# Moving a gather, a transposition, a few sums and one buffer across the seam between attention and a mixture of experts

## The chip, the cores and the metric

The kernel runs on one core of one Trainium2 chip. The metric is the device time of one execution in microseconds (us), the median of several runs. Times inside the execution come from one profiled run and count from its first instruction. The engines are called PE (TensorE; PEld is its weight load), DVE (VectorE), ACT (ScalarE), POOL (GpSimd) and SP (SyncE, which here only issues transfers).

## The reference

Attention without a softmax, then an RMS norm, then a mixture of experts in which each token goes to one of eight experts or is passed through unchanged.

```python
batch, n_heads, seq, head_dim = (8, 8, 576, 64)
kv = np.einsum('bhsd,bhse->bhde', k, v)
out = np.einsum('bhsd,bhde->bhse', q, kv)
rms = np.sqrt(np.mean(out * out, axis=-1, keepdims=True) + 1e-06)
attn = (out / rms * g_norm).astype(np.float32)
...
x = np.ascontiguousarray(attn.transpose(0, 2, 1, 3)).reshape(B * S, H * D)   # 4608 x 512
skip_score = x @ w_skip
do_compute = skip_score > 0
logits = xc @ w_gate
e_idx = np.argmax(logits, axis=1)
...
h = np.maximum(xc[mask] @ w1[e], 0.0)          # w1[e]: 512 x 1024, e of 8
y[mask] = gate_w[mask, None] * (h @ w2[e])     # w2[e]: 1024 x 512
out[do_compute] = xc + y
```

## The kernel before

**Attention.** The queries are worked through in 36 units. A unit is a batch b, a group i of four of the nine row columns of that batch, and a half u of the eight heads; the ninth columns of four batches together make two further units (i is `None`; these are units 16, 17 and, at the very end, 34, 35). The loop `for n in range(NU + 2)` is software-pipelined and written out by hand under a manual schedule, so each engine gets its instructions in the order of the code. In step n it turns the queries of unit n + 1 (`turn`, L432, bank `q_ps`), takes the root for unit n - 1 (`root`, L497, on ACT), multiplies unit n (`values`, L468 or L476, into a bank pair `o_ps`, or `sum_ps` for units 28, 31 and 34) and squares it (L482, ACT), sums the squares (`squares`, L490, DVE), and normalises unit n - 1 (`norm`: reciprocal L504, product `xl` L508, both DVE). Then `finish` gives POOL the small gate sums `lp` and `lg` (L525, L529, L533: skip score and eight logits of each token, carried through as nine extra columns) and puts the large product with g, `xb` (L538), into a list `late`. `scale` empties that list one step later, so in POOL's order xb(n) stands just before lp(n + 1); each xb waits for the reciprocal of the unit after it. `store_x` sends a finished xb to the output in HBM, half by POOL (L560, L566) and half by SP (L561, L570) for some groups, all by SP for the others. Jobs can be hung on a step with `at(step, part, job)`; the parts are "early", "pe", "dve" and "end".

**Ranking.** The tokens are ranked in three groups of tiles that end at 12, 22 and 36. For each group `choose` (DVE, L582 to L602) finds the expert of each token as a one-hot `ohb`, `rank` (PE, L612 to L618) counts, and `number` (DVE, L629 to L644) makes slot numbers: the high part `hi_k` and a one-hot of the low part, `oha_k`. After the second group the experts are ordered by how many tokens they have, and the weights of the first one are loaded (SP, L309 and L314). `columns` (DVE: `ohc` L659, `bv` L663) makes from `hi_k` the columns that `place` (PE, L672) multiplies with `oha_k`, so that each slot gets its token's row number in `srow`.

**The first slots.** The tokens of groups one and two come from batches 0 to 4, so the first 128 slots of the first expert are known before attention ends. `early` computes them: L757, L761 on DVE, 22 products on PE (L767, the job `put`), three small DVE operations (L771 to L776), and a gather of 128 rows from the output by POOL (L778) into `xg0`. It is a generator driven by the loop: `put` runs in the "pe" part of step 30, and the rest is issued in the "dve" part of that step.

**After attention** the pools of the attention are closed and the experts' pools opened on the same memory; a tile there waits for what used its room before. `bank` hands out seven PSUM banks in turn. The code at the seam is this:

```python
        expert_in(xg0, xt0, first)
        layer_1(0, xt0, ht0, slice(0, P), range(0, 5))
        rank(LAST)
        drain(number(LAST))
        layer_1(0, xt0, ht0, slice(0, P), range(5, FC))
        last_bv = columns(NE, NT - NE, colid_i, row_k, 2, slot_pool, NT // 2)
        settle(0, NE, first_bv)
        yps0 = layer_2(0, ht0, first, None, range(0, 3))
        settle(NE, NT, last_bv)
        layer_2(0, ht0, first, yps0, range(3, 5))
```

`expert_in` turns the 128 rows (L971 on PE, L974 on ACT), `layer_1` and `layer_2` are the expert's two products (L995, L1006; eight blocks each), and `settle` is `place` and two DVE additions (L735). With `srow` complete, POOL gathers the other rows of the first two experts (L961), PE repeats some slots (L914) and turns the rows, and the experts run one after another to the end: the first with plain products, the other seven with a seven-product scheme (L1074). SP loads the next expert's weights as rooms come free, POOL scatters the results (L1216).

## Time and profile before

| | us |
|---|---|
| runs | 400.13, 400.14, 398.63; median 400.13 |
| profiled execution, its own time | 399.31 |
| its span, first to last instruction | 397.4 |
| PE busy | 365.8 (92% of the span) |
| PEld, DVE, ACT, POOL busy | 317.8, 240.7, 144.0, 124.9 |
| mean granted PE clock | 0.973 |
| last attention product ends (L476) | 118.25 |
| first expert product begins (L995) | 122.56 |
| last slot products begin (L672, 14 of them) | 137.40 |
| first late gather begins (L961) | 139.04 |
| rest of layer one of the first expert begins | 145.94 |

A profile line in order of time has the start, the busy time, the engine, the line and operation, what is written from what, and in brackets how long the engine had been idle and what ended that ("<-"). If an instruction waits for several things, the profile names the one that came last by its records. The granted clock is the share of full speed at which PE was let run. The time of the execution exceeds the span by 1.9 us.

### The profile page before, as it was taken

To read this page: it belongs to the slowest core of one execution; us is meant where nothing else is said; L and a number is where in the kernel's file an instruction comes from. 1 tells how busy PE (TensorE), PEld (TensorE's weight loads), DVE (VectorE), ACT (ScalarE), POOL (GpSimd) and SP (SyncE) were. 2 spreads that over 40 slices of the span, in tenths; PEclk is the share of its full clock that TensorE was granted. 3 is DMA by queue.
4 is the path that set the end of the run, shared out by engine and by line. 5 is a ranking of instruction groups with operands and counts; after the bars stand their busy time and mean duration, and the time that the engine had idled before them with its cause. 6 is when DMAs were issued, how large, how long until landed. Compare 5 with 4: busy or idle time off the path is not lost.

```text
span 397.4 us, 9594 instructions
## 1 busy us (share of the span) xinstructions
PE 365.8 (92%) x3822; PEld 317.8 (80%) x3822; DVE 240.7 (61%) x615; ACT 144.0 (36%) x384; POOL 124.9 (31%) x197
## 2 busy tenths in 40 slices
PE   8789999899967889999999999999999989989991
PEld 4577988799857659579879978978988978979980
DVE  2333567577884651656756657857767756868711
ACT  2265786576862212113402421421431430421410
POOL 7023677565776270133012303203303203102001
PEclk9699999999996989999999999999999999999997
DMA  8999999985795249726516354663663572611001
GB/s 296 395 391 389 343 408 403 405 262 178 239 389 142 54 136 383 262 65 228 183 73 225 105 211 116 210 225 105 206 228 104 185 246 67 210 47 55 2 2 50
DMA packets 31544, 81.70 MB, mean 206 GB/s; under 512 B 2106, under 2 KB 2114, under 8 KB 31492
## 3 DMA queue, kind: packets, MB, share of 16 engines
q1 hardware_dynamic: 27456, 68.69, 49.6%
q0 software_dynamic: 4016, 12.31, 9.1%
q8 instruction: 32, 0.52, 0.6%
q14 instruction: 20, 0.16, 0.1%
q10 hardware_dynamic: 20, 0.02, 0.0%
HBM read 66.80 MB, written 14.48 MB: 205 GB/s over the span
## 4 chain that ended last, share of the span: by engine, by line
PE 56%; issue 17%; DMA 12%; POOL 5%; DVE 5%; ACT 2%; POOLq 0%; DVEq 0%; ACTq 0%
PE bank L1074 23%; DMA out_dram<-xg,rows 8%; PE bank L1006 6%; PE o_ps L468 6%; PE sum_ps L352 4%; PE q_ps L432 4%; PE bank L995 3%; DMA xg<-out_dram,asrc 2%; POOL xb L538 2%; PE g_ps L366 2%; DMA xg<-out_dram,src 2%; POOL out_dram L1216 1%; DVE xl L508 1%; PE bank L971 1%; POOL xg L961 1%
## 5 line engine op out<-in xcount | busy, mean ns | idle before, releaser
L1084 ACT COPY p<-bank 128x128 f32<-128x128 f32 (+6 forms) x70 | 20.8, 297 | 105.4 <-PE bank L1074 103.8
L1074 PE MATMUL bank<-xt,w 128*128 128x128 f32 (+5 forms) x336 | 55.5, 288 | 0.0
L538 POOL TENSOR_TENSOR xb<-xl,g_b 128x512 f32<-128x512 f32 x36 | 42.9, 1191 | 31.8 <-DVE rs L504 27.9
L1074 PEld LDWEIGHTS bank<-xt,w 128*128 128x128 f32 x336 | 47.0, 190 | 1.9 <-DVE bank L1078 1.2
L1078 DVE TENSOR_TENSOR bank<-bank,p 128x128 f32<-128x128 f32 (+6 forms) x70 | 23.6, 337 | 39.8 <-PE bank L1074 38.1
L1216 POOL DMA_INDIRECT out_dram<-xg,rows x16 | 16.2, 1013 | 76.9 <-DVE xg L1213 75.4
L468 PE MATMUL o_ps<-kvd,qT 128*128 128x146 f32 x240 | 36.2, 291 | 2.5 <-DVE xl L508 2.2
L1074 PE MATMUL bank<-xs,s 128*128 128x128 f32 (+5 forms) x224 | 36.7, 288 | 0.0
L1006 PE MATMUL bank<-w,ht 128*32 128x128 f32 (+2 forms) x448 | 36.6, 322 | 0.0
L468 PEld LDWEIGHTS o_ps<-kvd,qT 128*128 128x128 f32 x240 | 31.8, 190 | 4.1 <-ACT sq L482 1.6
L961 POOL DMA_INDIRECT xg<-out_dram,src x15 | 16.8, 1122 | 51.7 <-DMA out_dram<-xg,rows 29.0
L1216 POOL DMA_INDIRECT out_dram<-xg,arows x8 | 9.0, 1128 | 76.4 <-DVE xg L1213 76.1
L1074 PEld LDWEIGHTS bank<-xs,s 128*128 128x128 f32 x224 | 31.1, 190 | 1.0 <-ACT p L1084 0.8
L490 DVE TENSOR_REDUCE rs<-sq 128x8 f32<-128x512 f32 x36 | 24.5, 679 | 11.6 <-ACT sq L482 11.5
L1006 PEld LDWEIGHTS bank<-w,ht 128*32 128x32 f32 (+2 forms) x448 | 20.4, 121 | 13.6 <-issue 10.9
L508 DVE TENSOR_TENSOR xl<-o_ps,rs 128x584 f32<-128x584 f32 x33 | 25.3, 767 | 4.3 <-PE o_ps L468 0.5
L1074 PE MATMUL bank<-w,ht 128*128 128x256 f32 x112 | 27.2, 386 | 0.0
L1074 PE MATMUL bank<-t,ht 128*128 128x256 f32 x112 | 27.1, 385 | 0.0
L352 PE MATMUL sum_ps<-v,k 64*64 64x64 f32 x1152 | 25.3, 230 | 1.6 <-issue 1.5
L352 PEld LDWEIGHTS sum_ps<-v,k 64*64 64x64 f32 x1152 | 21.8, 141 | 4.7 <-issue 2.9
L1074 PE MATMUL bank<-t,hs 128*128 128x256 f32 x112 | 25.3, 379 | 0.0
L995 PE MATMUL bank<-xt,w 128*128 128x128 f32 (+1 forms) x128 | 23.2, 349 | 1.0 <-ACT xt L974 0.7
(199 smaller groups left out, 673.6 us busy)
## 6 DMA issues: line engine op xcount, KB each, us to landing
w<-in_moe_w_dram SPq DMA_DIRECT2D x16, 2048.0 KB, 10.5
q<-in_q_dram SPq DMA_DIRECT2D x8, 1152.0 KB, 9.2
k<-in_k_dram SPq DMA_DIRECT2D x7, 1152.0 KB, 12.7
v<-in_v_dram SPq DMA_DIRECT2D x7, 1152.0 KB, 13.4
out_dram<-xb SPq DMA_DIRECT2D x26, 256.0 KB, 8.7
out_dram<-xb POOLq DMA_DIRECT2D x10, 256.0 KB, 6.7
k<-in_k_dram SPq DMA_DIRECT2D x2, 576.0 KB, 5.2
v<-in_v_dram SPq DMA_DIRECT2D x2, 576.0 KB, 6.2
```

Of the source, the lines that this page charges most:

```text
L352: nc.tensor.matmul(out=sum_ps[w * 64:(w + 1) * 64, a, u, :], lhsT=kt[r, 2 * u + w, c, :], rhs=vt[r, 2 * u + w, c, :], start=(c == 0), stop ...
L468: nc.tensor.matmul(out=ps[:, w, 0:2 * PK].rearrange("p (r k) -> p r k", r=2)[:, :, cols], lhsT=qT[:, w, a, :], rhs=kvds[b % KVD][:, u, w, ...
L490: nc.vector.tensor_reduce(out=rs[:, :, :], in_=sq[:, :, :, :].rearrange("p x y (a d) -> p x (y a) d", a=2), axis=AX.X, op=ALU.add)
L508: nc.vector.tensor_tensor(out=xl[:, :, :, :].rearrange("p x y (a k) -> p x (y a) k", a=2), in0=ps[:, :, 0:2 * PK].rearrange("p x (h k) -> ...
L538: late.append((lambda: nc.gpsimd.tensor_tensor(out=xb[:, :, 4 * u * D:(4 * u + 4) * D].rearrange("p r (w x) -> p r w x", w=2), in0=xl[:, : ...
L961: nc.gpsimd.indirect_dma_start(out=x_of(xg, off, m), out_offset=None, in_=cut_rows(m)[:, :], in_offset=bass.IndirectOffsetOnAxis(ap=idx[:, ...
L995: nc.tensor.matmul(out=hps[:, cols], lhsT=w_sb[r][0][:, dc, f * P:(f + 1) * P], rhs=xt[:, dc, cols], start=(dc == 0), stop=(dc == DC - 1))
L1006: nc.tensor.matmul(out=yps[q * m:(q + 1) * m, 0:n], lhsT=ht[:, f, off:off + m], rhs=w_sb[r][1][:, f, q * n:(q + 1) * n], start=(f == 0), s ...
L1074: nc.tensor.matmul(out=out, lhsT=lhsT(i), rhs=rhs(i), start=start and i == 0, stop=i == k - 1, skip_group_check=True)
L1078: nc.vector.tensor_tensor(out=to, in0=x, in1=y, op=ALU.add)
L1084: nc.scalar.copy(out=t, in_=x)
L1216: ins = nc.gpsimd.indirect_dma_start(out=cut_rows(m)[:, :], out_offset=bass.IndirectOffsetOnAxis(ap=rows[:, col:col + 1], axis=0), in_=x, ...
```

## The change

Six things are edited.

1. The DVE operations and the POOL gather of `early` go into the job `put`, and `put` runs in a new part "mid" of step 30: right after `values`, ahead of `squares` and `norm`.
2. `expert_in` for the first slots goes. A job `first_in` at the end of step 35 turns the 128 rows into the bank `q_ps` and copies them to a tile of their own, `xt_first`, which layer one reads. Three banks are drawn and left unused before layer one. A block of zeros moves from its own tile into the first weights' room.
3. `norm` of the last unit no longer calls `scale`, so xb(34) comes after the gate sums of unit 35 on POOL. The last two xb now wait for the end of `choose` (`ohb`) instead of the reciprocal and `bv`.
4. `columns` is split into `hits` and `weighed`; for the first 22 tiles `hits` runs before `choose`, `weighed` after it.
5. Three stores move from POOL to SP: those of units 16 and 17, of the last batch's second group (32, 33), and of units 34 and 35.
6. The last columns (`last_bv`) are written into the pool `gat_pool`, in the tiles of the first columns, after `settle` of the first 22 tiles, instead of into `slot_pool` before it.

```diff
@@ -502,7 +502,8 @@
         nq, b, i, u = units[n]
         (ps, _), rs = ops.pop(n), rss.pop(n)
         inverse = nc.vector.reciprocal(out=rs[:, :, :], in_=rs[:, :, :])
-        scale(n, inverse)
+        if n < NU - 1:
+            scale(n, inverse)
         r4 = rs[:, :, :].unsqueeze(3)
         xl = att_pool.tile([P, 2, 2, PK], FP32, tag="xl", name="xl", bufs=4)
         nc.vector.tensor_tensor(
@@ -557,21 +558,24 @@
         xb = xbs.pop(nq)
         if i is None:
             rows = out.rearrange("(f hf r p c) d -> f hf p r c d", f=NF, hf=2, r=2, c=C)[b]
-            nc.gpsimd.dma_start(out=rows[0, :, :, C - 1, :], in_=xb[0:64, :, :])
-            return lambda: nc.sync.dma_start(out=rows[1, :, :, C - 1, :], in_=xb[64:128, :, :])
+            def store():
+                for hf in range(2):
+                    nc.sync.dma_start(out=rows[hf, :, :, C - 1, :], in_=xb[hf * 64:(hf + 1) * 64, :, :])
+            return store
         rows = out[b * S:(b + 1) * S, :].rearrange("(p c) d -> p c d", c=C)[:, 4 * i:4 * i + 4, :]
         rows = rows.rearrange("p (hf r) d -> hf p (r d)", hf=2)
         x = xb[:, :, :].rearrange("p r d -> p (r d)")
-        if i == 1:
+        first = int(i == 1 and b < B - 1)
+        if first:
             nc.gpsimd.dma_start(out=rows[0], in_=x[0:64, :])
 
         def store():
-            for hf in range(i, 2):
+            for hf in range(first, 2):
                 nc.sync.dma_start(out=rows[hf], in_=x[hf * 64:(hf + 1) * 64, :])
         return store
 
 
-    ohbs, rks = {}, {}
+    ohbs, rks, chosen = {}, {}, []
 
     def choose(g):
 
@@ -599,8 +603,9 @@
                                        op0=ALU.is_gt, op1=ALU.mult)
         yield
         ohb = gat_pool.tile([P, TG, E], BF16, tag="ohb", name="ohb")[:, 0:nt, :]
-        nc.vector.tensor_tensor(out=ohb, in0=eorder[:, :].unsqueeze(1).to_broadcast([P, nt, E]),
-                                in1=fi.unsqueeze(2).to_broadcast([P, nt, E]), op=ALU.is_equal)
+        chosen.append(nc.vector.tensor_tensor(
+            out=ohb, in0=eorder[:, :].unsqueeze(1).to_broadcast([P, nt, E]),
+            in1=fi.unsqueeze(2).to_broadcast([P, nt, E]), op=ALU.is_equal))
         ohbs[g] = ohb
         yield
 
@@ -651,20 +656,25 @@
         for _ in pieces:
             pass
 
-    counted = []
-
-    def columns(t0, nt, colid, val, pieces, pool, room):
+    def hits(t0, nt, colid, pool, room):
 
         ohc = pool.tile([P, room, NCOL], BF16, tag="ohc", name="ohc")[:, 0:nt, :]
         nc.vector.tensor_tensor(
             out=ohc, in0=colid[:, :].unsqueeze(1).to_broadcast([P, nt, NCOL]),
             in1=hi_k[:, t0:t0 + nt].unsqueeze(2).to_broadcast([P, nt, NCOL]), op=ALU.is_equal)
+        return ohc
+
+    def weighed(ohc, t0, nt, val, pieces, pool, room):
+
         bv = pool.tile([P, room, pieces, NCOL], BF16, tag="bv", name="bv")[:, 0:nt, :, :]
-        counted.append(nc.vector.tensor_tensor(
+        nc.vector.tensor_tensor(
             out=bv, in0=ohc.unsqueeze(2).to_broadcast([P, nt, pieces, NCOL]),
             in1=val[:, t0:t0 + nt, :].unsqueeze(3).to_broadcast([P, nt, pieces, NCOL]),
-            op=ALU.mult))
+            op=ALU.mult)
         return bv
+
+    def columns(t0, nt, colid, val, pieces, pool, room):
+        return weighed(hits(t0, nt, colid, pool, room), t0, nt, val, pieces, pool, room)
 
     def place(ps, bv, t0, nt, first=True, last=True):
 
@@ -747,6 +757,17 @@
 
 
     xg0 = keep.tile([P, CK, DM], FP32)
+    xt_first = keep.tile([P, DC, P], FP32)
+
+    def first_in():
+
+        xp = ps_q.tile([P, 512], FP32, tag="q", name="q_ps")
+        xp = xp[:, :].rearrange("p (j t) -> p j t", t=P)
+        for j in range(DC):
+            nc.tensor.transpose(out=xp[:, j, :], in_=xg0[:, 0, j * P:(j + 1) * P],
+                                identity=ident[:, :])
+        nc.scalar.copy(out=xt_first[:, :, :], in_=xp)
+
     KNOWN = (ends[LAST - 1] - 2) // 4 * S
     assert ends[LAST - 1] == 4 * (KNOWN // S) + 2
     NE = ends[LAST - 1]
@@ -766,30 +787,29 @@
             for t in range(NE):
                 nc.tensor.matmul(out=ps, lhsT=oha_k[:, t, :], rhs=bv[:, t, :], start=(t == 0),
                                  stop=(t == NE - 1), skip_group_check=True)
-        yield put
-        row = gat_pool.tile([P, 1], FP32, tag="row1", name="row1")
-        nc.vector.tensor_reduce(out=row[:, :], in_=ps, axis=AX.X, op=ALU.add)
-        src = keep.tile([P, 1], I32, name="src1")
-
-        nc.vector.tensor_scalar(out=row[:, :], in0=row[:, :], scalar1=float(N), scalar2=None,
-                                op0=ALU.add)
-        nc.vector.scalar_tensor_tensor(out=src[:, :], in0=row[:, :], scalar=float(N), in1=row[:, :],
-                                       op0=ALU.is_lt, op1=ALU.mult)
-        nc.gpsimd.indirect_dma_start(
-            out=xg0[:, 0, :], out_offset=None, in_=out[0:KNOWN, :],
-            in_offset=bass.IndirectOffsetOnAxis(ap=src[:, 0:1], axis=0))
+            row = gat_pool.tile([P, 1], FP32, tag="row1", name="row1")
+            nc.vector.tensor_reduce(out=row[:, :], in_=ps, axis=AX.X, op=ALU.add)
+            src = keep.tile([P, 1], I32, name="src1")
+            nc.vector.tensor_scalar(out=row[:, :], in0=row[:, :], scalar1=float(N), scalar2=None,
+                                    op0=ALU.add)
+            nc.vector.scalar_tensor_tensor(out=src[:, :], in0=row[:, :], scalar=float(N),
+                                           in1=row[:, :], op0=ALU.is_lt, op1=ALU.mult)
+            nc.gpsimd.indirect_dma_start(
+                out=xg0[:, 0, :], out_offset=None, in_=out[0:KNOWN, :],
+                in_offset=bass.IndirectOffsetOnAxis(ap=src[:, 0:1], axis=0))
+        yield "mid", put
 
     load_kv(1)
     load_kv(2)
     load_q(1)
 
 
-    zero = setup.tile([64, DM], FP32)
-    nc.gpsimd.memset(zero[:, :], 0.0)
+    zero = room[0:64, 4 * DM:5 * DM]
+    nc.gpsimd.memset(zero, 0.0)
     for b in range(KNOWN // S // 4 * 4, KNOWN // S):
         nc.gpsimd.dma_start(
             out=out[b * S:(b + 1) * S, :].rearrange("(p c) d -> p c d", c=C)[:, C - 1, :],
-            in_=zero[:, :])
+            in_=zero)
 
     starts = {}
     for n, (_, b, i, _) in enumerate(units):
@@ -824,6 +844,7 @@
             yield from early()
 
     streams = []
+    at(NU - 1, "end", first_in)
 
     PACE = (2, 4)
     for n in range(NU + 2):
@@ -834,6 +855,7 @@
         jobs(n, "early")
         if n < NU:
             values(n)
+        jobs(n, "mid")
         if THIRD + 2 <= n < NU:
             squares(n)
         done = norm(n - 1) if 1 <= n <= NU else None
@@ -843,9 +865,10 @@
         if done:
             done()
         if n == NU:
+            ohc = hits(0, NE, colid_i, gat_pool, NE)
             drain(choose(LAST))
-            first_bv = columns(0, NE, colid_i, row_k, 2, gat_pool, NE)
-            scale(NU, counted[-1])
+            scale(NU, chosen[-1])
+            first_bv = weighed(ohc, 0, NE, row_k, 2, gat_pool, NE)
         jobs(n, "dve")
 
         if n in ends[:LAST]:
@@ -853,7 +876,8 @@
         for pace, stream in streams:
             for job in itertools.islice(stream, pace):
                 if job:
-                    at(n + 1, "pe", job)
+                    part, job = job if isinstance(job, tuple) else ("pe", job)
+                    at(n + 1, part, job)
                     break
         jobs(n, "end")
     for _, stream in streams:
@@ -1318,13 +1342,14 @@
         plan[0] = plan[0][1:]
         xt0, ht0 = new_xt(), new_ht()
         blank(ht0, 0)
-        expert_in(xg0, xt0, first)
-        layer_1(0, xt0, ht0, slice(0, P), range(0, 5))
+        for _ in range(3):
+            bank()
+        layer_1(0, xt_first, ht0, slice(0, P), range(0, 5))
         rank(LAST)
         drain(number(LAST))
-        layer_1(0, xt0, ht0, slice(0, P), range(5, FC))
-        last_bv = columns(NE, NT - NE, colid_i, row_k, 2, slot_pool, NT // 2)
+        layer_1(0, xt_first, ht0, slice(0, P), range(5, FC))
         settle(0, NE, first_bv)
+        last_bv = columns(NE, NT - NE, colid_i, row_k, 2, gat_pool, NE)
         yps0 = layer_2(0, ht0, first, None, range(0, 3))
         settle(NE, NT, last_bv)
         layer_2(0, ht0, first, yps0, range(3, 5))
```

## The prediction

> **What bounds the kernel now.** I read the page first, then busy time by stretch, then the instructions in order of time between 113 and 138 us, where every part of the change lies.
>
> ```profile
> PE 365.8 (92%) x3822; PEld 317.8 (80%) x3822; DVE 240.7 (61%) x615; ACT 144.0 (36%) x384; POOL 124.9 (31%) x197
> PEclk9699999999996989999999999999999999999997
> ```
>
> TensorE is busy 92% of the span, so a gain can come only from its gaps or from time at a low clock. The clock row (tenths, 40 slices of 9.9 us) has its one deep notch, a 6, in slice 13: 119 to 129 us, where attention ends and the experts begin. By stretch (columns: busy us of PE, PEld, DVE, ACT, POOL with counts, granted clock, DMA share, GB/s):
>
> ```profile
> 113.50:118.30 4.80, 2.72 (x72) 2.26 (x72) 3.98 (x10) 2.03 (x6) 4.38 (x7) 1.00 1.03 395
> 118.30:120.80 2.50, 0.01 (x1) 0.04 (x1) 2.33 (x5) 0.90 (x2) 2.42 (x5) 0.78 0.72 287
> 120.80:126.40 5.60, 4.92 (x22) 4.53 (x23) 0.90 (x2) 0.89 (x3) 4.80 (x11) 0.50 0.74 192
> 133.00:140.00 7.00, 5.47 (x37) 2.82 (x34) 2.67 (x9) 1.73 (x2) 0.96 (x1) 1.00 0.23 61
> ```
>
> PE stands still from 118.3 to 120.8, works at half clock until 126.4, and idles again after 133. POOL has no free time from 113.5 to 126.4. In order of time:
>
> ```profile
> 113.14 1.07 POOL L778 DMA_INDIRECT xg<-out_dram,src  x1 [0.78 <-DVE rs L504]
> 119.92 0.77 DVE L508 TENSOR_TENSOR xl<-sum_ps,rs 128x584 f32<-128x584 f32 x1
> 120.79 1.09 PE L971 MATMUL bank<-ident,xg 128*128 128x128 f32 x4 [2.54 <-DVE rs L504]
> 120.93 0.77 DVE L508 TENSOR_TENSOR xl<-o_ps,rs 128x584 f32<-128x584 f32 x1
> 122.56 6.61 PE L995 MATMUL bank<-xt,w 128*128 128x128 f32 x40 [0.68 <-ACT xt L974]
> 123.39 0.58 POOL L566 DMA_DIRECT2D out_dram<-xb  x1 [0.30 <-POOL xb L538]
> 124.20 1.18 POOL L538 TENSOR_TENSOR xb<-xl,g_b 128x512 f32<-128x512 f32 x1
> 126.01 0.22 POOL L533 TENSOR_TENSOR lg<-lp 128x18 f32<-128x18 f32 x1
> 127.70 0.27 DVE L602 TENSOR_TENSOR ohb<-eorder,fi 128x112 bf16<-128x112 f32 x1
> 129.00 0.38 PE L612 MATMUL g_ps<-top,ident 128*128 128x120 f32 x2
> 129.97 1.19 POOL L538 TENSOR_TENSOR xb<-xl,g_b 128x512 f32<-128x512 f32 x1 [3.74 <-DVE bv L663]
> 130.51 0.68 DVE L637 TENSOR_SCALAR lo_i<-s_i 128x14 int32<-128x14 int32 x1
> 131.46 0.66 POOL L560 DMA_DIRECT2D out_dram<-xb  x1 [0.30 <-POOL xb L538]
> 135.64 0.51 DVE L659 TENSOR_TENSOR ohc<-colid_i,hi_k 128x336 bf16<-128x336 int32 x1 [2.32 <-issue]
> 137.40 0.51 PE L672 MATMUL g_ps<-bv,oha_k 128*128 128x48 bf16 x14 [1.53 <-DVE srow L735]
> ```
>
> The view of line 778 gives the gather 7.3 us from issue to landing, so the rows were there at 120.44. The transposes (L971) began at 120.79, after both that landing and the xl of unit 34 (120.69), which frees their PSUM bank. Expert layer one (L995, first five blocks) ran 122.56 to 129.00. The gate sums (L533) ended at 126.23, their choice (ohb, L602) at 127.97: rank (L612) waited for layer one, not for it, with 1.0 us to spare. Last, the second columns (L659) started at 135.64, after the stores of L561 and L560 had landed (views of these lines: 3.4 and 3.9 us, so 134.6 and 135.36), and PE idled 1.53 us for them. From 137.40 a row runs to the last gathers (L961, 139.04 on) and the rest of layer one (145.94); all of it hangs on 137.40.
>
> [...] 0.5 from 119.70 to 126.53 and from 147.01 to 150.43, two windows and one. The window before the first drop held 22% PE work, that before the second 54%; one with 58% (112.9 to 116.3) brought none. [...] lo_i (L637) took 0.68 us, ending at 131.19 as xb ends at 131.16; hi_k, alike in shape, took 0.16. [...] The trace has 7.3 for 256 KB in a saturated stretch (DMA share 1.03), and I use that.
>
> **Part by part.** "Unit n" is an attention step; 36 of them, the last 34 and 35.
>
> *Gather sooner.* Three VectorE ops (0.15, 0.15, 0.16 us) and the gather move from after norm(29) to before squares(30). PE's puts end at 109.44, so src is ready near 110.05 and the gather issues near 110.4 instead of 113.14. VectorE's squares(30) and xl(29) slip 0.6 us, and PE's values(32) from 111.44 to about 111.85; but values(33) waits for xl(30) (113.56) and values(35) for xl(32) (117.36), fed by squares that wait for ScalarE, and the three ops are gone from behind: nothing at the end. On POOL the gather (1.07) passes xb(28), lp and lg of 29, and lies where POOL idled 1.74 and 0.78 us: POOL is 0.7 us earlier from 114 on. Landing: 110.4 + 7.3 = 117.7. Bounds: 114 (an unhindered transfer, 3.5 from the 139.04 gather) to 120.4 (moved only when the queues drain, as before).
>
> *Turned inside the attention.* Four transposes and a copy move to the end of step 35, in the free q bank: 118.35 to 118.95, copy (ScalarE, 0.58) to 119.7. The copy stands ahead of root(35), which ran at 119.72 waiting for rs until then: free, unless the gather is late (below). Layer one does not start at once, though: in the built program its first block takes the bank that xl(34) frees (120.69) and the second the one of xl(35) (121.70). So it starts at 120.8, not 122.56.
>
> *The clock decides what that is worth.* Full-speed work of the five blocks: 3.97 us at half clock plus 2.47 = 4.46. (a) Same window edges: the transposes lift 116.3 to 119.7 from 22% to 40%, under the 54% that still dropped; half clock until 126.53 does 2.87, the rest ends at 128.1: 0.9 us won. (b) Edges such that one window's length of half clock meets layer one: 4.46 + 1.7 from 120.8, end 127.0: 2.0 won. (c) No drop: second block from 121.8, end 125.4; then the choice bounds: 3.2 won.
>
> *Gate sums ahead.* POOL drops the L566 store (0.9 with its wait) and passes lp/lg(35) ahead of xb(34) (1.17); with the 0.7 above, lg ends near 123.4 instead of 126.23, ohb 1.74 later, near 125.2. The hits (0.70) go into VectorE's 4.57 us idle[...]. In (a) and (b) this is under layer one and worth nothing by itself; it keeps rank from becoming the wait. Both xb now wait for ohb and contend with bv (1.26): ends 127.8 to 129.0. They have behind them on POOL only a memset, and VectorE's lo_i, which is not due before 128.5.
>
> *SP's stores.* Three issues (0.6 each) move to SP, whose queue stands empty here; the last two go out at 129.1 and 129.7 and land by 133.1. The first L961 gather needs them; it is due 1.64 after the last place, near 136: covered by 2.9 us. Without that cover, their lateness counts fully.
>
> *Another room.* The last columns go to gat_pool, behind VectorE's own work and PE's 22 places. From rank on PE has work for 135.86 - 129.00 = 6.86 us until it needs bv; VectorE needs some 2.95 to oha's end, then waits for the places, and adds, ohc, bv are 0.4 + 0.5 + 0.9 = 1.8 beside 2.82 of PE work. So the 1.53 idle goes, whichever clock. In (c) VectorE's chain, held by xb, ends about 133.2 and caps the whole gain at 4.3.
>
> *Sum.* (a) 0.9 + 1.5 = 2.4; (b) 2.0 + 1.5 = 3.5; (c) 4.3. Between (a) and (b): 3.0, and what follows hangs on it. The profiled execution took 399.31 us (span 397.4, 1.9 around it); the median shown is 400.13, the mean of all four 399.55. I subtract from the mean: 396.5.
>
> **Rivals.**
> - *Full clock, or the second drop goes.* A shift moves PE's idle windows against the edges; the half clock after 147.01 costs 1.7. For it: the 54% and 58% windows lie close. Then 399.55 - 3.5 - 1.7 = 394.3; (c) alone 395.2.
> - *The gather gains nothing.* If rows move only when the queues drain at 120.4, layer one starts as before and 1.5 remains: 398.0. For it: no packet of POOL's queue moved between 111 and 117.4. Against it: POOL's store issued at 103.33 moved from 107.0 under the same load.
> - *Slower: a late gather holds ScalarE.* The copy in front of root(35) stops recip, xl(35), lp, choice. Landing at L, layer one ends at about L + 8.5, as before from 120.44; with the 1.5 won elsewhere it decides from L = 122.0, slower past 0.5% from 124. The longest store of this stretch took 14.2 us; that would be 124.6 and 402.2. Against it: the gather had 7.3, the POOL stores 6.2.
>
> **The numbers.** Forecast (a to b, 395.8 to 397.6) 0.50; full clock or second drop gone (393.5 to 395.7) 0.23; no gain from the gather (397.6 to 399.5) 0.20; slower 0.07. Range 394.0 to 398.8: leaves out some 0.05 below, 0.12 above. About 0.5%, 2 us, is what a measurement of this kernel can tell from no change, so faster means under 398.1: 0.50 + 0.23 + a little of the third = 0.74; same 0.19; slower 0.07.
>
> **What would show it.** Gather issued near 110.4, landed before 118.3; transposes right behind 118.3; layer one from 120.8; ohb before 126; rank start 127 to 128.5; no idle before the 14 places of L672's successor; L961's first gather near 136 with no DMA wait. Wrong if layer one still starts after 122, if rank waits for ohb, or if the first late gather waits for the last stores.

## The result, and the profile after

| us | before | changed |
|---|---|---|
| median (runs) | 400.00 (12) | 396.38 (12) |
| lowest to highest | 398.63 to 402.55 | 393.03 to 399.36 |
| profiled execution: its own time, span | 399.31, 397.4 | 395.03, 393.1 |

The changed kernel takes 0.9903 of the time of the kernel before, with a 95% interval of 0.9876 to 0.993. That is faster by the forecast's bound of 0.5%, and the forecast of 396.5 lies 0.1 us beside the median. So close a hit is partly luck: the forecast took 3.0 us off a mean of 399.55, while the medians fell by 3.6 from 400.00; in a second set of executions (e12 below, 396.33 against 399.36) they fell by 3.0.

The page of the changed kernel answers the two lines shown of before. TensorE's busy time hardly differs; the notch of 6 tenths has become an 8.

```profile
PE 364.3 (93%) x3822; PEld 316.9 (81%) x3822; DVE 241.4 (61%) x615; ACT 144.6 (37%) x384; POOL 124.7 (32%) x194
PEclk9999999999998999999999999999999999999997
```

The two executions can't be compared by the clock on the wall: in the changed one all of attention ends 2.08 us later (the last attention product at 120.33 instead of 118.25). About 1.5 of that is there soon after the start, where full clock came at 23.44 us instead of 20.72 (eight products of L468 took 2.15 us at 21.03, 1.17 at 24.81); the last 0.55 comes between 63 and 71 us, and its cause stays open. All times below therefore count from the end of that product, written "+". In order of time the changed kernel's seam reads:

```profile
112.46 1.08 POOL L797 DMA_INDIRECT xg<-out_dram,src  x1 [1.80 <-DVE src L795]
...
120.26 0.66 PE L767 MATMUL q_ps<-ident,xg 128*128 128x128 f32 x4
120.96 0.59 ACT L769 COPY xt_first<-q_ps 128x512 f32<-128x512 f32 x1
122.01 0.77 DVE L509 TENSOR_TENSOR xl<-sum_ps,rs 128x584 f32<-128x584 f32 x1
122.88 6.12 PE L1019 MATMUL bank<-xt_first,w 128*128 128x128 f32 x40 [1.96 <-ACT rs L497]
123.70 1.26 DVE L662 TENSOR_TENSOR ohc<-colid_i,hi_k 128x528 bf16<-128x528 int32 x1
125.70 0.22 POOL L534 TENSOR_TENSOR lg<-lp 128x18 f32<-128x18 f32 x1
127.40 0.28 DVE L606 TENSOR_TENSOR ohb<-eorder,fi 128x112 bf16<-128x112 f32 x1
127.75 3.28 POOL L539 TENSOR_TENSOR xb<-xl,g_b 128x512 f32<-128x512 f32 x2 [1.82 <-DVE ohb L606]
128.83 0.38 PE L617 MATMUL g_ps<-top,ident 128*128 128x120 f32 x2
131.06 1.29 SPq L563 DMA_DIRECT2D out_dram<-xb  x2
135.53 0.52 PE L682 MATMUL g_ps<-bv,oha_k 128*128 128x48 bf16 x14
137.19 1.05 POOL L985 DMA_INDIRECT xg<-out_dram,src  x1 [6.04 <-DVE src L754]
```

The transposes (L767) follow the last attention product at once, and layer one (L1019) starts at +2.55 instead of +4.31, 0.1 us after the product xl of unit 34. The rank (L617) starts at +8.50 instead of +10.75, the last 14 places (L682) at +15.20 instead of +19.15, without a bracket, so without idle time. The gap of 2.5 us in front of the transposes and the one of 1.5 in front of the places are gone; one of 1.96 is left in front of layer one. Its bracket names a root on ScalarE that ended at 122.10; the product xl, which frees the bank that layer one writes to, ended last, at 122.78. The hits (L662) took 1.26 us where the same operation took 0.70 before, beside xb and the gate sums on GpSimd, and the two last xb, beside bv (1.25), took 3.28 together (1.18 and 1.19 before).

The spans differ by 4.3: -2.1 for the later start, +3.8 at the seam (rest of layer one at +23.93 instead of +27.69), +1.7, half of 3.42 us, because the second half clock of before (147.01 to 150.43) didn't come, and about 0.9 in later gaps. Of these only the 3.8 can be laid to the change, and about 1.3 of it hangs on the clock: in e7 below, which has two windows of half clock at the seam as the kernel before has, the rest of layer one begins at +25.21.

### The profile page after: what moved, and what is told of

Same layout as the page of the kernel before. It is cut to its first block, busy times and chain, and to the rows that moved or that the text cites. A ratio compares the mean times of both kernels' runs of the same rounds, so it can differ in the third digit from the quotient of the medians.

```text
span 393.1 us, 9589 instructions
## 1 busy us (share of the span) xinstructions
PE 364.3 (93%) x3822; PEld 316.9 (81%) x3822; DVE 241.4 (61%) x615; ACT 144.6 (37%) x384; POOL 124.7 (32%) x194
## 4 chain that ended last, share of the span: by engine, by line
PE 65%; issue 12%; DMA 10%; DVE 5%; ACT 3%; POOL 2%; ACTq 0%; POOLq 0%; DVEq 0%
PE bank L1098 30%; PE bank L1030 8%; PE o_ps L468 6%; DMA out_dram<-xg,rows 6%; PE bank L1019 5%; PE sum_ps L352 4%; PE q_ps L432 4%; PE g_ps L366 2%; DMA xg<-out_dram,src 2%; DMA xg<-out_dram,asrc 2%; PE bank L995 1%; DVE xl L509 1%; DMA w<-in_g_norm_dram 1%; DVE rs L490 1%; PE g_ps L384 1%
## 5 line engine op out<-in xcount | busy, mean ns | idle before, releaser
L539 POOL TENSOR_TENSOR xb<-xl,g_b 128x512 f32<-128x512 f32 x36 | 43.7, 1216 | 29.5 <-DVE rs L504 27.5
L468 PE MATMUL o_ps<-kvd,qT 128*128 128x146 f32 x240 | 36.9, 296 | 2.4 <-DVE xl L509 1.1
L468 PEld LDWEIGHTS o_ps<-kvd,qT 128*128 128x128 f32 x240 | 32.5, 193 | 4.1 <-DVE xl L509 2.1
L1098 PEld LDWEIGHTS bank<-t,ht 128*128 128x128 f32 x112 | 20.8, 190 | 4.1 <-issue 1.6
```

Of the source, the lines that this page charges most:

```text
L468: nc.tensor.matmul(out=ps[:, w, 0:2 * PK].rearrange("p (r k) -> p r k", r=2)[:, :, cols], lhsT=qT[:, w, a, :], rhs=kvds[b % KVD][:, u, w, ...
L539: late.append((lambda: nc.gpsimd.tensor_tensor(out=xb[:, :, 4 * u * D:(4 * u + 4) * D].rearrange("p r (w x) -> p r w x", w=2), in0=xl[:, : ...
L1098: nc.tensor.matmul(out=out, lhsT=lhsT(i), rhs=rhs(i), start=start and i == 0, stop=i == k - 1, skip_group_check=True)
```

## The experiments

Every execution is placed by the same marks. "Windows" is the number of stretches of 3.41 us at half clock around the seam; "ohb product" is the rank's first product that needs the choice, 0.22 us behind the rank's start where it doesn't wait; "tail" is from TensorE's last product to the end.

| kernel | windows | layer one | ohb product | 14 places | rest of layer one | tail | median | ratio, interval |
|---|---|---|---|---|---|---|---|---|
| before | 2 | +4.31 | +10.97 | +19.15 | +27.69 | 8.7 | 400.00 | 1 |
| changed | 1 | +2.55 | +8.72 | +15.20 | +23.93 | 8.8 | 396.38 | 0.9903 (0.9876 to 0.993) |
| e12 changed again | 1 | +2.54 | +8.82 | +15.30 | +23.83 | 8.7 | 396.33 | 0.9925 (0.9902 to 0.9949) |
| e1 old room | 1 | +2.54 | +8.81 | +15.29 | +23.82 | 7.2 | 392.64 | 0.9872 (0.9807 to 0.9937) |
| e7 old room again | 2 | +2.54 | +10.20 | +16.68 | +25.21 | 7.3 | 393.71 | 0.9831 (0.9774 to 0.9888) |
| e2 room alone | 3 | +4.29 | +11.35 | +17.83 | +26.38 | 9.0 | 397.34 | 0.9937 (0.9916 to 0.9958) |
| e3 turned late | 2 | +4.30 | +10.69 | +17.17 | +25.72 | 8.5 | 396.68 | 0.9935 (0.9911 to 0.9959) |
| e4 sums behind | 2 | +2.54 | +10.03 | +16.51 | +25.05 | 8.5 | 395.24 | 0.9894 (0.9869 to 0.9919) |
| e8 gathered late | 2 | +4.01 | +10.86 | +17.34 | +26.10 | 8.7 | 396.48 | 0.9889 (0.984 to 0.9938) |
| e5 three blocks in q | 1 | +1.26 | +7.67 | +14.33 | +22.88 | 9.1 | 394.19 | 0.9831 (0.9782 to 0.988) |
| e6 PE kept busy | 0 | +2.54 | +7.40 | +14.40 | +22.92 | 8.6 | 394.59 | 0.9841 (0.9791 to 0.9892) |
| e11 e6, sums behind | 0 | +2.54 | +8.57 | +15.05 | +23.59 | 8.5 | 393.73 | 0.9846 (0.9806 to 0.9886) |
| e9 two more instructions | 1 | +2.54 | +8.91 | +15.39 | +23.96 | 7.4 | 394.82 | 0.9898 (0.9852 to 0.9943) |
| e10 joined | 0 | +1.26 | +7.39 | +14.32 | +22.84 | 9.3 | 394.02 | 0.9854 (0.9812 to 0.9897) |

The medians come from four sets of executions, each with its own executions of the kernel before, against which the ratio is taken: their medians are 400.00 for changed, 399.51 for e1 to e4, 400.14 for e5 to e8 and 399.36 for e9 to e12. The marks come from one execution of each kernel. They repeat within 0.2 us where the windows are equal (changed, e12, e1, e9), while single runs of the changed kernel differ by up to 6 us. So the marks decide below, and the medians only where their intervals lie apart.

**e1 and e7: the last columns back in their old room.** The experiment undoes edit 6:

```diff
-        settle(0, NE, first_bv)
-        last_bv = columns(NE, NT - NE, colid_i, row_k, 2, gat_pool, NE)
+        last_bv = columns(NE, NT - NE, colid_i, row_k, 2, slot_pool, NT // 2)
+        settle(0, NE, first_bv)
```

> The changed kernel with one part undone: the last columns go into the other pool again, ahead of the additions for the first 22 tiles. Measured on the interval from the end of the last attention product to the start of the 14 last slot products (19.15 us in the kernel before, 15.20 in the changed one). Theory (the room is worth the wait for the last stores): those stores were issued at 131.06 and 131.7 and landed at 135.0 in the changed kernel's profile; ohc then starts near 135.3 and bv ends near 136.7, so the interval grows by 1.2 to 16.4, PE idles 1.2 before the products, and the median is about 397.6. Rival (PE has enough other work, the room hides nothing): 15.2 and 396.4.

The columns didn't wait, and the places had no idle time before them (e1, in order of time):

```profile
132.12 0.72 PE L682 MATMUL g_ps<-bv,oha_k 128*128 128x48 bf16 x22
132.95 0.50 DVE L662 TENSOR_TENSOR ohc<-colid_i,hi_k 128x336 bf16<-128x336 int32 x1
135.34 0.51 PE L682 MATMUL g_ps<-bv,oha_k 128*128 128x48 bf16 x14
```

The theory fell: `ohc` began at +12.90, before the first of the two last stores landed at +14.03, while in the kernel before it began only after both had landed. The likely reason is the layout. By the addresses of the built programs, which no trace holds, `ohc` begins at byte 210304 of each partition in the kernel before, and the xb of units 34 and 35 holds bytes 206880 to 210976, so the first writer waits for the last two stores. Edit 2 adds `xt_first`, 2048 bytes, below both, and takes away the zeros' tile, also 2048 bytes, below xb alone. So in e1 xb stays in place and `ohc` begins at 212352, clear of it. No run has edit 2 alone, so that it is this edit is argued, not shown. The median was 3.7 us below the changed kernel's, which neither theory had. Four runs are few; e7 is the same kernel with six more.

> The same kernel as e1_room_back (the last columns again in the pool and at the place in the order that they had before the change), with more runs. Theory (with the room of the turned rows and the zeros moved, the last columns' old room no longer lies under the last two stores, so that the new room adds nothing): TensorE again without idle time ahead of the 14 places, which start 6.7 us after the rank, and a median like the changed kernel's, 395.7 to 396.9. Rival (the old room is better than the new one, as the first four runs suggest): 393 to 394.

The seam is again no better than the changed kernel's (+16.68 with two windows; from the ohb product to the places 6.48, as in the changed kernel), but the tail is 7.3 instead of 8.8 and the median is again low, 393.71. e9 below deals with the tail.

**e2: the new room alone, in the kernel before.**

```diff
-        last_bv = columns(NE, NT - NE, colid_i, row_k, 2, slot_pool, NT // 2)
         settle(0, NE, first_bv)
+        last_bv = columns(NE, NT - NE, colid_i, row_k, 2, gat_pool, NE)
```

> The kernel before with this one part alone: the last columns in the first columns' tiles, after the additions for the first 22 tiles. Theory: the 1.53 us idle before the 14 products goes, interval 19.15 - 1.5 = 17.6, median 400.0 - 1.5 = 398.5. Rival (it is worth something only together with the earlier gate sums, since the additions then stand in the way of ohc on VectorE): interval 19.1, median 400.0.

From the ohb product to the places it took 6.48 us instead of 8.18: 1.70 won, the idle 1.53 and a little overlap. So in the kernel before the room is worth what was forecast; in the changed one it is worth nothing, since the same wait is gone without it. The median fell further than the 1.5 us expected, to 397.34 (1.7 to 3.4 us by the interval), although this execution had three windows. By the medians alone e2 can't be told from the changed kernel, whose intervals overlap with its own: that the other edits add to the room rests on the marks.

**e3 and e8: half of the gather's change each.** e3 takes `first_in` out and calls `expert_in` after attention as before; e8 puts the three VectorE operations and the gather back behind norm of unit 29 and keeps the turn inside.

```diff
-    at(NU - 1, "end", first_in)
...
-        layer_1(0, xt_first, ht0, slice(0, P), range(0, 5))
+        expert_in(xg0, xt0, first)
+        layer_1(0, xt0, ht0, slice(0, P), range(0, 5))
```

> The changed kernel with the transposes of the first slots moved back behind attention (bank, copy and tile as in the kernel before); the gather stays early, and so do the gate sums and the room. Theory (transposes and copy lay on the path between the freed bank and layer one): layer one starts 4.3 us after the last attention product instead of 2.55, and the half clock lasts longer, so rank starts 10 to 10.7 after it instead of 8.5; the interval is 17 to 17.5, the median 398 to 398.6. Rival (the early gather alone made the gain, it no longer matters where the rows are turned): interval 15.2, median 396.4.

> The changed kernel with its gather of the first slots' rows, and the three VectorE operations before it, back where they stood before the change; the transposes stay inside the attention. Theory (ScalarE's copy of the turned rows stands ahead of the root of unit 35 and holds it when the gather is late): the gather lands about 2.2 us after the last attention product, transposes behind it, copy at 2.9 to 3.5, so xl of unit 35 ends near 4.9 instead of 3.45, ohb near 8.8 instead of 7.34, rank at 9.5 to 10, the 14 places 6.7 behind it; median 397.5 to 398.3. Rival (ScalarE isn't on the path, layer one alone waits): rank at 9.0 or less, ohb unchanged, median 396.4 to 397.

Layer one starts at +4.30 in e3, as before: the early gather without the early turn gains 0.01. In e8 it starts at +4.01: the early turn without the early gather gains 0.3. Together they gain 1.77. In e8, in order of time:

```profile
122.77 1.11 PE L767 MATMUL q_ps<-ident,xg 128*128 128x128 f32 x4 [2.22 <-DMA xg<-out_dram,src]
123.92 0.58 ACT L769 COPY xt_first<-q_ps 128x512 f32<-128x512 f32 x1 [2.66 <-PE q_ps L767]
124.40 0.30 ACT L497 ACTIVATE rs<-rs,eps_t 128x8 f32<-128x8 f32 x1
125.07 0.77 DVE L509 TENSOR_TENSOR xl<-o_ps,rs 128x584 f32<-128x584 f32 x1
128.67 0.28 DVE L606 TENSOR_TENSOR ohb<-eorder,fi 128x112 bf16<-128x112 f32 x1
```

The bracket of L767 shows the gather's landing as what ended TensorE's idle time, at +2.2. The copy (L769) holds the root of unit 35 (L497) behind it on ScalarE; so its xl ends at +5.29 instead of +3.45 and ohb at +8.40 instead of +7.34. The copy thus holds the chain to the choice, as expected. But the rank did not wait for the choice. Layer one began at +4.01, when the late rows had been copied (+3.95), and ended under two windows at +10.81, 2.4 us after ohb. In this execution the late gather cost time through layer one alone, as the rival has it, and the hold on ScalarE was hidden behind that. In e3 the marks came as expected (places at +17.17). The medians did not: 396.48 for e8 and 396.68 for e3, not 397.5 to 398.6. Set beside e7, which has two windows like them, e3 is 0.5 and e8 0.7 later at the places; beside the changed kernel's execution with one window they are 2.0 and 2.1 later. Which of the two distances the mean over many executions has, the profiles can't tell; the medians lie nearer to the smaller.

**e4: xb of unit 34 ahead of the gate sums again.**

```diff
-        if n < NU - 1:
-            scale(n, inverse)
+        scale(n, inverse)
```

> The changed kernel with xb(34) ahead of the gate sums of unit 35 on GpSimd again; only xb(35) waits for the choice. Theory (the sums were not on the path while the half clock holds layer one): the choice ends 1.2 us later, 8.55 after the last attention product instead of 7.35, just where rank stands (8.5): interval 15.2 to 15.6, median 396.4 to 396.8. Rival (each us of GpSimd's queue is a us of the kernel): interval 16.4, median 397.6.

ohb ended at +8.46 instead of +7.34, and layer one, under two windows, at +9.97. The rank waited for layer one. The places came at +16.51, where the rival has 16.4, but that is the second window's doing: e7, also with two, has +16.68. The sums' order is worth nothing here, as forecast; with one window layer one ends at +8.66 to +8.86 (changed, e12, e1, e9), still 0.2 us or more behind such an ohb. The median, 395.24, lies 1.2 below the expected range.

**e6 and e11: TensorE kept busy.** Five products go ahead of the last attention product and six behind the transposes; nobody reads them. e11 is e6 with e4's edit.

```diff
+    def keep_warm(ps, n):
+        for _ in range(n):
+            nc.tensor.matmul(out=ps, lhsT=ones[:, :],
+                             rhs=ones[:, :].unsqueeze(1).to_broadcast([P, 4, P]), start=True, stop=True,
+                             skip_group_check=True)
```

> The changed kernel with 11 spare bf16 products of 128x512 whose results nobody reads, five behind the last-but-one attention product and six behind the transposes, only to fill the idle time of TensorE around the end of the attention. Theory (the half clock comes from TensorE's idle windows there): no half clock between 0 and 9 us after the last attention product; layer one still starts near 2.6, its five blocks take 4.5 us, so they end near 7.1 and the rank is held by the choice, at 7.4 to 7.7 instead of 8.50; the 14 places at 14.1 to 14.4; median 394.7 to 395.4. Rival (the clock drops for another reason, or the spare products delay the attention's own): the half clock stays, rank at 8.4 or later, median 396.4 or more.

> The kernel of e6 (TensorE kept busy, so that no half clock covers the choice) with the product xb of unit 34 again ahead of the gate sums of unit 35 on GpSimd. Theory (the order of GpSimd's work is worth nothing while the half clock holds layer one, but once that is gone the choice holds the rank): ohb ends 8.4 to 8.5 after the last attention product instead of 7.34, the rank follows it at 8.5 to 8.6 instead of 7.18, the 14 places at 15.2 to 15.4, median 0.8 to 1.1 above e6's, about 395.5. Rival (the rank can wait, something later holds): the 14 places at 14.4 as in e6, median as e6's.

The half clock went. By stretch (columns as in the prediction: PE, PEld, DVE, ACT, POOL, granted clock, DMA share, GB/s), first the changed kernel, then e7, then e6, each cut into the clock's stretches of 3.41 us in its own trace:

```profile
119.01:122.42 3.41, 1.33 (x36) 1.04 (x36) 3.11 (x7) 1.94 (x5) 3.25 (x8) 1.00 0.96 374
122.42:125.84 3.42, 2.96 (x14) 2.99 (x15) 2.41 (x4) 0.28 (x1) 3.11 (x8) 0.50 0.64 175
125.84:129.25 3.41, 3.41 (x35) 3.41 (x35) 2.71 (x7) 1.05 (x4) 1.59 (x2) 1.00 0.60 132
```

```profile
120.00:123.42 3.42, 2.68 (x12) 2.71 (x13) 2.72 (x4) 0.28 (x1) 3.18 (x8) 0.50 0.63 171
123.42:126.83 3.41, 3.41 (x18) 3.41 (x17) 2.71 (x7) 0.56 (x2) 1.51 (x3) 0.50 0.70 154
```

```profile
118.97:122.38 3.41, 3.04 (x44) 1.54 (x42) 3.11 (x7) 1.72 (x5) 3.23 (x7) 1.00 0.99 370
122.38:125.79 3.41, 3.18 (x27) 3.18 (x28) 2.28 (x5) 0.68 (x3) 3.00 (x7) 1.00 0.65 178
```

A window with 1.33 us of TensorE work (39%) is followed by one at half clock; where that one holds 2.96 us (87%) the clock is back, where it holds 2.68 (78%) another follows. In e6 these windows hold 3.04 and more, and nothing drops at the seam; a window of half clock still came at 142.86. Layer one's five blocks then take 4.80 us instead of 6.12 and end together with the choice, at +7.34. With the choice later, it is the bound, as e11 shows:

```profile
129.46 0.28 DVE L605 TENSOR_TENSOR ohb<-eorder,fi 128x112 bf16<-128x112 f32 x1
129.78 0.21 PE L619 MATMUL g_ps<-ohb,ut 128*128 128x112 bf16 x1 [1.01 <-DVE ohb L605]
136.26 0.52 PE L681 MATMUL g_ps<-bv,oha_k 128*128 128x48 bf16 x14
```

The product waits 1.01 us for ohb, at +8.57 instead of e6's +7.40, and the places come 0.65 later. So the order of the sums is worth something only without the half clock. The medians of e6 and e11 don't tell them apart (ratios 0.9841 and 0.9846; 393.73 for e11, not the 395.5 expected), and e11 had no half clock behind the seam. Of e6's gain 0.5 is given back by VectorE: `oha_k` takes 3.04 us there instead of 2.09, beside the last xb on GpSimd, and TensorE idles 0.36 before the places (7.00 from the ohb product to them, not 6.48).

**e5: three blocks of layer one inside attention,** in the free bank q.

```diff
+    at(NU - 1, "end", first_layer)
+    at(NU, "end", first_relu)
...
-        layer_1(0, xt_first, ht0, slice(0, P), range(0, 5))
+        layer_1(0, xt_first, ht0, slice(0, P), range(3, 5))
```

> The changed kernel, but the first three blocks of expert layer one go into the free q bank right behind the transposes, still inside the attention, so that they no longer wait for the bank that the product xl of unit 34 frees. Theory (that bank is what holds layer one, and half clock eats part of it): layer one starts some 1.5 us after the last attention product instead of 2.55; the five blocks end about 1 us sooner and the rank is then held by the choice (ohb, which ends 7.34 after the last attention product): rank at 7.5 to 7.8 instead of 8.50, the 14 places at 14.2 to 14.5 instead of 15.19, median 395.0 to 395.7. Rival (the half clock moves with the work, or the choice was the bound all along): rank not before 8.4, median 396.4.

Layer one starts at +1.26 and, even with a window of half clock, its five blocks end 0.3 after the choice; the places come at +14.33, and the median, 394.19, lies 0.8 below the expected range. The bank that xl of unit 34 frees was the bound of layer one's start.

**e9: VectorE's program two instructions longer.**

```diff
         nc.vector.tensor_single_scalar(out=colid[:, :], in_=colid_i[:, :], scalar=-CK, op=ALU.add)
+        nc.vector.tensor_single_scalar(out=colid[:, :], in_=colid_i[:, :], scalar=-CK, op=ALU.add)
+        nc.vector.tensor_single_scalar(out=colid[:, :], in_=colid_i[:, :], scalar=-CK, op=ALU.add)
```

> The changed kernel with one tiny VectorE operation of the seam issued three times instead of once: two more instructions in VectorE's program, and no tile or room moved. Theory (the gain of the old room in e1 and e7 has nothing to do with the room: VectorE's program is two instructions longer there[...]): no gap in VectorE's last waits, 7.1 to 7.4 us from TensorE's last product to the end instead of 8.8, median about 1.5 below the changed kernel's in this call. Rival (the rooms in memory make the difference): 8.4 to 9.1 us from the last product to the end, and the changed kernel's median.

> The changed kernel once more, unedited, as the measure for the other three on the same chip. Expected: 395.7 to 396.9, a gap of about 2 us in VectorE's last waits, 8.4 to 9.1 us from the last product to the end, and the 14 places 15.2 us after the last attention product if the half clock there lasts one window, 16.6 if it lasts two.

The engines' last waits, in the views of one line (count, durations in ns, first and last start), first e12's, then e9's:

```profile
L1385 DVEq EVENT_SEMAPHORE  x13: 21/50/50, 384.0 to 390.8; - x13
L1385 ACTq EVENT_SEMAPHORE  x12: 38/38/38, 387.5 to 388.4; - x12
```

```profile
L1387 DVEq EVENT_SEMAPHORE  x13: 21/50/50, 384.3 to 389.2; - x13
L1387 ACTq EVENT_SEMAPHORE  x12: 38/38/38, 388.1 to 388.9; - x12
```

The last scatter is issued at 384.31 in e12. ScalarE starts the last of its waits at 388.4, VectorE 2.4 us later, and the end follows; in e9 the two are 0.3 apart. In the changed kernel VectorE pauses there for 2.2 us (388.95 to 391.12), and in that pause, at 389.94, the queue that the trace calls q14, instruction, moved a packet of 8 KB. From 375 us on that queue moved six packets of 8 KB in the changed kernel and e12, five in e1, e7 and e9. That VectorE waited for the packet is not shown. The tail is 7.4 instead of 8.7, as in e1 and e7 (7.2 and 7.3), whose VectorE program is also two instructions longer: their traces hold 776 VectorE instructions like e9's, those of the kernels whose VectorE stops hold 773 to 775. So the old room's shorter tail goes with the two instructions, not with memory, which e9 leaves as it is. The medians, 394.82 and 396.33, stand as expected, though their intervals overlap. Of the old room's surplus in the medians (1.2 to 3.8 us, by the ratios of e1 and e7 against the two of the changed kernel) the tail explains about 1.5; the rest is not explained.

**e10: all of it joined.** e5's blocks, e6's first five spare products, ten small ones between the turns of the late rows, and one instruction more for VectorE.

```diff
-        for piece in plan[0]:
+        for piece, n in zip(plan[0], (4, 6, 0)):
             landed = expert_in(xg0, xt0, piece)
+            for _ in range(n):
+                nc.tensor.matmul(out=g_ps[:, 0:256], lhsT=ones[:, :],
```

> The changed kernel with all that the runs pointed to: the first three blocks of layer one inside the attention (e5), five spare products in TensorE's pause ahead of the last attention product and ten small ones between the turns of the late rows, to keep its clock up, and VectorE's program at the length of e1's. Theory ([...]the rank stays held by the choice): no half clock from the last attention product on, rank at 7.4 to 7.6, the 14 places at 14.2 to 14.5, the rest of layer one at 22.7 to 23.0 after the last attention product, 7.1 to 7.4 us from the last product to the end, median 391.5 to 393. Rival (the parts don't add up, since spare products delay the rows' turns or the choice holds everything): 394 or more.

All marks of the seam came as expected, and no half clock fell on it or behind it until TensorE was done. The tail did not (9.3):

```profile
L1416 PEldq EVENT_SEMAPHORE  x13: 51/51/51, 383.0 to 391.0; - x13
L1416 DVEq EVENT_SEMAPHORE  x13: 21/50/50, 383.8 to 388.5; - x13
```

VectorE, with 776 instructions here too, was done at 388.6, 0.3 after ScalarE, as in e9. Now it was TensorE, its program 15 products longer, that stopped for 2.4 us among its last waits. Whether the 15 products brought that stop was not tried by itself. The median of 394.02 missed the expected 391.5 to 393 and lies where the rival has it. It beats the kernel before, and the changed one by e12's interval, just (upper end of the ratio 0.9897 against 0.9902; 2.3 us below e12 on the same chip); with the first interval of the changed kernel it overlaps. The same holds for e5, e6, e7 and e11. None of the five is shown to be better than another. The seam itself is close to the bound of the choice: e5, e6 and e10 agree within 0.1 at the places.

## Why the prediction was right, point by point

- *Gather sooner.* Right: src released it at the equivalent of 110.38 in before's times (forecast 110.4), and it landed in 7.2 us. The rival "gains nothing until the queues drain" is out.
- *Turned inside the attention.* Right to the tenth: +2.55 is 120.80 in before's times, and e5 shows that the bank was the bound. The earlier start of layer one needs both halves (e3, e8).
- *The clock.* That its edges can fall differently was the author's assumption; in the runs half clock began at +1.45 before (119.70), +2.09 in the changed kernel (122.42) and +1.80 in e7 (120.00). Case (b) occurred in the profile; layer one's end, forecast at 127.0, was at +8.67, so 126.92. The other cases exist in its variants: the places come 2.47 earlier than before with two windows (e7, edit 6 undone; forecast (a) 2.4), 3.95 with one (forecast (b) 3.5) and 4.75 with none (e6, only with the unread products; forecast (c) at most 4.3). The small surplus is in the room's term (1.70 instead of 1.53) and, in (b), 0.25 in the rank's. (c) was capped by VectorE's chain, slower beside xb (`oha_k` 3.04 us in e6, 2.09 without xb beside it), as the text said, 0.5 us sooner than it said.
- *Gate sums.* Right: ohb ended at +7.34 (forecast near +6.95 and before +7.75), worth nothing under half clock (e4), and what keeps the rank from waiting without it (e11). Mis-sized: the hits, 0.70 in the forecast, took 1.26 beside an xb; in e8, with no xb beside them, they took 0.70.
- *SP's stores.* Right: issued at +10.73 and +11.37 (forecast +10.85 and +11.45), landed 3.3 us later near +14.7, 2.2 us ahead of the first late gather, which waited for its row numbers alone. No run undoes edit 4 or 5 alone, so what each adds is not shown.
- *Another room.* The idle time went, but the step credits it to edit 6, and it is gone without edit 6 as well (e1, e7), by the layout most likely through edit 2. The sum holds because a wait can be removed only once, which is luck. The prediction had put edit 2's moves of memory at nothing and had not looked at what else lay on the shifted rooms.
- *The rivals.* The second half clock vanished in this profile and stayed in e4, e6 and e7, so the first rival's 1.7 is a matter of phase. The late gather's rule held in e8: the landing L is +2.2, and layer one ended at +10.81 where L + 8.5 gives +10.7; the delay came through layer one's late start, with the held choice behind it. L stayed below the deciding point of +3.75, so e8 isn't slower than before.
- *Readings of the lines.* Three were too strong, and none enters the sum. POOL was not without free time from 113.5 to 126.4: its columns add up to 11.60 of 12.90 us. The clock row has a second 6, in slice 2, near the program's start. And the store issued at 103.33 moved from 107.4, not 107.0.

## What to carry to other kernels

Count from the last common event, not from the start, when single executions scatter more than the change is worth; the parts then repeat to 0.2 us. A wait on reused memory may hang on the layout rather than on the line that waits (in e1 `ohc` began at +12.90, ahead of the first store's landing at +14.03): a tile moved elsewhere may take it away, so look at both programs' waits before crediting an edit. And half clock can eat most of an earlier start: with two windows layer one began 1.77 us sooner and the rank's ohb product came only 0.77 sooner (e7). A few unread products in its pauses (e6, places at +14.40) bought as much as moving real work did (e5, +14.33).

## What the runs showed of the hardware

- The clock dropped after windows that were far from idle. From full clock, a window with 39% TensorE work was followed by half clock (changed, 119.01), in the kernel before one with 54% was too (143.60), and one with 58% was not (112.88). From half clock, a window with 78% kept it and one with 87% ended it (e7 at 120.00, changed at 122.42). These are no thresholds. In the same profiles a window of 77% was followed by half clock (e12 at 5.23, first pair of lines below), and one with 87% kept half clock (the kernel before at 13.89, second pair). So the busy share alone does not decide it, and what else counts is open.

```profile
5.23:8.64 3.41, 2.62 (x83) 2.22 (x82) 0.92 (x7) 0.72 (x3) 2.88 (x6) 1.00 1.05 399
8.64:12.05 3.41, 2.20 (x72) 2.04 (x72) 3.15 (x38) 0.44 (x2) 0.17 (x1) 0.50 1.05 392
```

```profile
13.89:17.31 3.42, 2.96 (x14) 2.77 (x14) 0.00 (x0) 0.54 (x2) 0.00 (x0) 0.50 1.04 394
17.31:20.72 3.41, 3.41 (x16) 2.13 (x15) 0.00 (x0) 2.09 (x6) 0.00 (x0) 0.50 1.05 391
```

- An engine can stop among its last waits. VectorE, or in e10 TensorE, stopped there for 1.8 to 2.5 us in eleven of the fourteen profiles, and the tail was 8.5 to 9.3 us there and 7.2 to 7.4 in the other three (e1, e7, e9). With two VectorE instructions more the stop was gone and the tail 7.4 (e9); with fifteen products more TensorE stopped for 2.4 us and the tail was 9.3 (e10). What an engine waits for in that stop is not shown; the packets of the queue called instruction (from 375 us on six of 8 KB in the kernel before and the changed one, five in e1, e7 and e9) differ along with it. These waits stand at the loop for further rounds of slots (L1385), around which the engines branch; whether the number of instructions or the place of that branch decides was not tried.
